# One-hot products on half the rows, with an even and an odd token side by side

## The chip, the cores and the metric

The kernel runs on one core of a Trainium2 chip. The metric is the device time of one execution in microseconds. A core has a matrix engine (PE, with its weight loads listed as PEld), a vector engine (DVE), a scalar engine (ACT), a general engine (POOL) and a queue engine (SP) that issues most transfers. All engines run on their own, each in the order of its own instruction stream, and wait for each other through semaphores.

## The reference

The input is 2048 tokens of 512 numbers. They are normalised, and two branches are added to them.

```python
xn = _layernorm(x, axis=-1)
return x + _A_ref(xn, ...) + _B_ref(xn, ...)

# A: attention, 32 query heads of 16, one shared head of keys and values
scores = einsum("bhqd,bkd->bhqk", q, k) * Dh ** -0.5
o = einsum("bhqk,bkd->bhqd", softmax(scores), v)

# B: product-key experts, 32 heads, 64 x 64 = 4096 experts
s1, s2 = q1 . k1, q2 . k2             # 64 scores each, per token and head
top_s, top_e = best 2 of the 2 x 2 sums of the two best of s1 and of s2
g = softmax(top_s)
act = gelu(einsum("nd,nhkd->nhk", xf, u[top_e]))
out = einsum("nhk,nhk,nhkd->nd", g, act, v[top_e])
```

A token uses 32 x 2 = 64 experts out of 4096. If many tokens choose, it can be cheaper to treat branch B as a dense product with a sparse gate matrix: G[token, expert] is the gate where the token chose the expert, and zero elsewhere.

## The kernel before

**Two halves of branch B.** The tokens are four groups of 512. For the first two groups (1024 tokens) the kernel gathers the rows of u and v of each chosen expert by indirect transfers (512 slots of 128 rows); DVE makes the dot product with the token (L991) and adds the weighted row to the token's total (L1026). For the last two groups it works densely (`dense`, L653): all 4096 experts in 32 blocks of 128, with matmuls pact (L733) for the activations and pout (L864) for the sums. These need the gate matrix, transposed: per block, 128 experts by 512 tokens.

**How the gates are made.** A token has 64 chosen experts. Expert e is split into a row a (0 to 127) and a block b (0 to 31), so that its gate matrix is a 128 x 32 table A^T B: A has for each of the 64 choices a one-hot row of length 128, and B a one-hot row of length 32 times the gate. The gate, scaled by 8192, is held as two f16 numbers, a high part and a remainder, so the 64 choices become 128 rows: rows 0 to 63 with the high parts, rows 64 to 127 with the remainders, and the same one-hot rows twice. `batch` (L563 on) fills three tiles `df1` (row a), `df2` (block b) and `dgt` (gates), token by token, on POOL and DVE. `spread` (L755) turns each into columns: four PE transposes of 128 x 128 into PSUM (ptd, L758) and one ACT copy to f16 into `tr` (L759). `onehot` (L782) makes, for a group of 16 tokens, the one-hot rows on DVE: a wide compare (L786, 128 x 2048), a narrow compare (L788, 128 x 512) and a multiply with the gates (L789). Then PE makes one product per token, 128 rows, 128 columns of weights, 32 streamed columns (pg, L818), all 16 tokens into one PSUM tile. Two ACT copies (L823) move that tile into a staging tile `gst`, and every 64 tokens SP stores it (L828, L830). The 512 tokens of a stage are 32 groups. The rows are prepared two groups ahead.

**What sets the order.** From the start of attention on, the order in which the instructions stand is written out by hand in one loop of rounds (`for d in range(half + 24)`). A round makes four pairs of score matmuls sc (L327) with four exponentials on ACT (L330), and 16 pv instructions (L341) for the four exponentials of the round before. There are 256 such rounds. Between the second and the third pair `mid` puts the copies of the one-hot products, the tanh of the gather part, and the dots and adds of gathered rows. At the end of a round `fill` runs the score thread: a generator that makes the expert scores psc (L531) and the dense work, and that yields a planned cost after each piece (UNIT 0.235 per matmul, 2.0 per one-hot group, 0.45 per `spread`). It is run until its cost so far reaches an aim which rises in equal parts over the 256 rounds, up to FILL. So a round holds about 3.6 units of the thread. `dense_on` tells the loop which part of the dense work is under way; while the one-hot groups run it is 2, and then the gather part advances by 1.4 slots a round.

**Buffers.** PSUM tiles of the tag x (3 buffers) serve psc, pact, pout, ptd and pg. The score tiles have two buffers of their own, so the third score pair of a round needs the first exponential to be done.

Of the kernel before, what the change touches and what calls it, by code (L numbers as in the profile page):

```python
# [23 lines left out]
P = 128  # L24
# [20 lines left out]
FILL = 948.0  # L45
# [10 lines left out]
def tile_kernel(ctx, tc, x, wq, wkv, wo, wqT, kT, uv, ub, vb, out):  # L56
# [500 lines left out]
    def dense_tiles():  # L557
        for _ in range(2):
            da = big.tile([P, 2, D], F32, name="da", tag="da", bufs=2)
            for i in range(2):  # L560
                DT.append(da[:, i, :].rearrange("p (t r s) -> p t r s", t=GT, r=2))

    def batch(ph, c, b):  # L563
# [60 lines left out]
        df1, df2, dgt = DT[:3]  # L624
# [12 lines left out]
        for r in range(2):  # L637
            G_.tensor_add(df1[:, :, r, w], hi, ii[:, 0])

        def gates():  # L640
            V.tensor_scalar(den, ex, 2.0, 2.0, op0=OP.mult, op1=OP.add)
            gg = T("gd", F32, [P, BT, 8])
            gv = gg.rearrange("p t (h k) -> p t h k", k=2)
            V.reciprocal(gv[:, :, :, 0], den)
            V.tensor_mul(gv[:, :, :, 1], ex, gv[:, :, :, 0])
            gh = T("gh", F16, [P, BT, 8])
            V.tensor_scalar(gh, gg, GS, None, op0=OP.mult)
            V.tensor_copy(dgt[:, :, 0, w], gh)
            stt(dgt[:, :, 1, w], gg, GS, gh, op0=OP.mult, op1=OP.subtract)
            if c == NC - 1:  # L650
                gated_all.append(True)
# [4 lines left out]
    def dense(DG, after):  # L656
# [62 lines left out]
        NQ = 512 // TB  # L719
# [7 lines left out]
        df1, df2, dgt = DT[:3]  # L727
# [27 lines left out]
        def spread(n):  # L755
            p = xtile("ptd")
            for j in range(GT):
                nc.tensor.transpose(p[:, j * P:(j + 1) * P], DT[n][:, j].rearrange("p r s -> p (r s)"), ident)  # L758
            nc.scalar.copy(tr[:, n, :], p)  # L759
# [3 lines left out]
        tr = kt(F16, (P, 3, 512))  # L763
# [9 lines left out]
        spread(2)  # L773
        yield 0.45
# [6 lines left out]

        def onehot(q):  # L782
            if q < NQ:
                tb = q * TB
                oa = kt(F16, shape(P))
                nc.vector.tensor_tensor(out=oa, in0=num(P), in1=bc(0, tb, P), op=OP.is_equal)  # L786
                ob = obs[:, q % 3]
                nc.vector.tensor_tensor(out=ob, in0=num(NB), in1=bc(1, tb, NB), op=OP.is_equal)  # L788
                nc.vector.tensor_mul(ob, ob, bc(2, tb, NB))  # L789
                OH[q] = oa, ob  # L790
# [15 lines left out]
        obs = kt(F16, (P, 3, TP, NB, 2))  # L806
        onehot(0)
        yield from rest_of_first
        onehot(1)
        for q in range(NQ):  # L810
            t0, ql = q // 4 * 64, q % 4
            if ql == 0:
                st = [late[0].tile([P, 16, 64], F32, name="gst", tag="wd", bufs=4) for _ in range(2)]
            onehot(q + 2)
            oa, ob = OH.pop(q)
            p = xtile("pg")
            for i in range(TB):
                nc.tensor.matmul(p[:, i * NB:(i + 1) * NB], oa[:, i // 2, :, i % 2], ob[:, i // 2, :, i % 2], start=True, stop=True)  # L818
            pv_ = p.rearrange("p (t b) -> p b t", b=NB)

            def copies(pv_=pv_, st=st, ql=ql, t0=t0):
                for hb in range(2):
                    nc.scalar.copy(st[hb][:, :, ql * TB:(ql + 1) * TB], pv_[:, 16 * hb:16 * hb + 16, :])  # L823
                if ql == 3:
# [14 lines left out]
            if q in (NQ - 16, NQ - 12):  # L839
                later_split((NQ - 16, NQ - 12).index(q))  # L840
            if q == NQ - 3:
                on_act(lambda: halves.__setitem__(2, half_split(2, 0)))
            if q == NQ - 3:
                quiet[0] = 3
            if q == NQ - 2:
# [3 lines left out]
            if q == NQ - 1:  # L849
                later_split(3)  # L850
            yield 2.0
# [519 lines left out]
```

## Time and profile before

| | before |
|---|---|
| median of 3 runs | 1915.84 us (1914.55 to 1916.74) |
| the profiled execution | 1914.46 us, span 1912.7 us |
| granted PE clock, mean | 0.984 |
| first one-hot stage | 32 groups, within 610.0 to 704.9 us |
| second one-hot stage | 32 groups, within 1409 to 1513.4 us |

The span runs from the first to the last instruction. In a row of a group, the words are line, engine, operation, output and input tiles, shapes and count, then the busy time in us and the mean of one in ns, then the idle time of the engine just before them and what ended it. In a row of windows stand the stretch, its length, busy time and count per engine, the granted clock as a share of full, the DMA share and GB/s. A row of the chain gives start, length and what ran. In a row of the timeline the start and length of a merged run of equal instructions stand first. In a row of waits stand total us, times and the longest.

### The profile page before, as it was taken

The page shows a single profiled execution, that of the slowest core. Times are in us where ns is not written, and L with a number is a line of the kernel's source. Part 1 is how long each engine was busy: PE and PEld are TensorE (multiplying, and loading weights), DVE is VectorE, ACT ScalarE, POOL GpSimd, SP SyncE. Part 2 cuts the span into 40 slices and gives each one's busy share as a digit, 9 for nine tenths or more (in the row PEclk, how much of TensorE's full clock was granted, in tenths as well). Part 3 has the DMA queues.
Part 4 walks back from the last instruction along what each step waited for, and adds up shares of the span by engine and source line. Part 5 has one row for each costly group of instructions (what it writes and reads, how often), then busy time and mean ns, then how long its engine had stood idle before and what let it go on. Part 6 is the DMA issues. An engine that isn't in the chain of part 4 may idle for free.

```text
span 1912.7 us, 35007 instructions
## 1 busy us (share of the span) xinstructions
PE 1824.5 (95%) x10990; PEld 956.9 (50%) x10990; DVE 1632.6 (85%) x6381; ACT 1290.5 (67%) x1803; POOL 693.8 (36%) x920
## 2 busy tenths in 40 slices
PE   6879999999999889999999999999998899999998
PEld 4544444555555334555555554555543345555553
DVE  6626887889998986999999897899989879999994
ACT  2336666655557987777887555555579877878873
POOL 1202433335443223344443354344522134444430
PEclk9989999999999989999999999999999999999999
DMA  7856878888673668899899987877636778899982
GB/s 263 303 201 223 289 263 299 279 290 297 223 261 122 220 222 270 247 280 296 262 288 301 377 284 241 290 248 260 237 114 228 264 227 292 269 286 279 287 274 83
DMA packets 245724, 489.76 MB, mean 256 GB/s; under 512 B 93972, under 2 KB 106644, under 8 KB 245532
## 3 DMA queue, kind: packets, MB, share of 16 engines
q0 software_dynamic: 73728, 268.47, 42.2%
q1 hardware_dynamic: 170568, 218.18, 34.8%
q8 instruction: 88, 1.44, 0.3%
q10 hardware_dynamic: 1236, 0.82, 0.1%
q14 instruction: 104, 0.85, 0.1%
HBM read 426.49 MB, written 55.61 MB: 252 GB/s over the span
## 4 chain that ended last, share of the span: by engine, by line
PE 78%; DVE 8%; ACT 2%; DMA 2%; issue 2%; SPq 0%; ACTq 0%; DVEq 0%
PE pv L341 21%; PE psc L531 18%; PE sc L327 15%; PE pact L733 9%; PE pout L864 9%; DVE oh L786 3%; PE pwo L434 2%; ACT pt L330 2%; PE pw L487 1%; DVE xa L1026 1%; DVE g L991 1%; DVE oh L789 1%; DVE oh L788 1%; DMA wqt<-in_wqT_dram 1%; DMA wk<-dw 1%
## 5 line engine op out<-in xcount | busy, mean ns | idle before, releaser
L330 ACT ACTIVATE pt<-sc 128x1024 f32<-128x1024 f32 x1024 | 994.4, 1028 | 445.7 <-PE sc L327 386.8
L979 POOL DMA_INDIRECT g<-in_uv_dram,idx x512 | 556.1, 1086 | 994.0 <-DVE xa L1026 520.2
L341 PE MATMUL pv<-pt,vaug 128*32 128x512 f32 x4096 | 505.3, 611 | 0.0
L327 PE MATMUL sc<-qa,kaug 64*128 64x512 f32 x2048 | 389.6, 453 | 15.6 <-ACT pt L330 13.3
L531 PE MATMUL psc<-wk,xt 128*128 128x512 f32 x1536 | 389.3, 401 | 4.8 <-DVE wk L497 3.6
L1026 DVE SCALAR_TENSOR_TENSOR xa<-g,w,xa 128x512 f32<-128x512 f32 x512 | 371.8, 744 | 0.1
L991 DVE CUSTOM_DVE_ANT_0 g<-g,xa 128x512 f32<-128x512 f32 x512 | 335.4, 681 | 7.0 <-DMA g<-in_uv_dram,idx 6.6
L531 PEld LDWEIGHTS psc<-wk,xt 128*128 128x128 f32 x1536 | 278.2, 188 | 108.5 <-issue 40.2
L327 PEld LDWEIGHTS sc<-qa,kaug 64*128 64x128 f32 x2048 | 158.3, 186 | 337.4 <-ACT pt L330 207.3
L341 PEld LDWEIGHTS pv<-pt,vaug 128*32 128x32 f32 x4096 | 108.2, 110 | 248.8 <-issue 247.1
L546 DVE FIND_INDEX8 i<-m,psc 128x8 uint32<-128x64 f32 x1024 | 206.4, 221 | 0.0
L733 PE MATMUL pact<-xt,wk 128*128 128x512 f32 x768 | 196.1, 400 | 0.0
L864 PE MATMUL pout<-wk,wd 128*128 128x512 f32 x768 | 194.9, 402 | 0.2 <-DVE wd L922 0.2
L544 DVE MAX8 m<-psc 128x8 f32<-128x64 f32 x1024 | 146.2, 214 | 38.7 <-PE psc L531 34.9
L864 PEld LDWEIGHTS pout<-wk,wd 128*128 128x128 f32 x768 | 140.8, 188 | 47.5 <-DVE act L991 5.5
L733 PEld LDWEIGHTS pact<-xt,wk 128*128 128x128 f32 x768 | 139.3, 188 | 48.5 <-issue 17.4
L698 DVE TENSOR_TENSOR wk<-rw,wk 128x512 fp32r<-128x512 f32 x128 | 84.9, 683 | 8.1 <-ACT wk L697 8.1
L867 DVE TENSOR_TENSOR da<-da,pout 128x512 f32<-128x512 f32 x128 | 82.8, 679 | 9.9 <-PE pout L864 9.8
L786 DVE TENSOR_TENSOR oh<-oh 128x2048 f16<-128x2048 f16 x64 | 78.0, 1219 | 0.6 <-ACT pt L330 0.4
L697 ACT CAST wk<-rw 128x512 fp32r<-128x512 f32 x128 | 74.0, 632 | 0.0
L546 DVE MATCH_VALUE_LOAD i<-m,psc 128x8 f32 x1024 | 71.0, 69 | 0.0
L590 POOL CAST fi<-i 128x64 f32<-128x64 uint32 x32 | 8.5, 266 | 152.9 <-DVE i L546 152.0
(159 smaller groups left out, 1343.4 us busy)
## 6 DMA issues: line engine op xcount, KB each, us to landing
wk<-dw SPq DMA_DIRECT2D x96, 512.0 KB
wqt<-in_wqT_dram SPq DMA_DIRECT2D x32, 512.0 KB
dw<-wk SPq DMA_DIRECT2D x32, 512.0 KB
rw<-in_ub_dram SPq DMA_DIRECT2D x64, 256.0 KB
rw<-in_vb_dram SPq DMA_DIRECT2D x64, 256.0 KB
gy<-dg SPq DMA_DIRECT2D x64, 256.0 KB
qa<-dqh SPq DMA_DIRECT2D x128, 64.0 KB
g<-in_uv_dram,idx POOLq DMA_INDIRECT x512
```

Of the source, the lines that this page charges most:

```text
L327: nc.tensor.matmul(p[:, b, :], kaug[o:o + 64, kc * P:(kc + 1) * P], QA[u][o:o + 64, i, :], start=True, stop=True)
L330: nc.scalar.activation(pt, p, AF.Exp, scale=SCALE)
L341: nc.tensor.matmul(PV[u][32 * j:32 * j + 32, :], vaug[:, kc, :], pt[:, b, :], start=kc == 0, stop=kc == 15)
L531: nc.tensor.matmul(p, XT[k][:, a, j * P:(j + 1) * P], WC[n_][k][:, bb, :], start=n == 0, stop=n == 11)
L544: nc.vector.max(m8[:, jb, s, :], p[:, s * E:(s + 1) * E])
L546: nc.vector.max_index(i8[:, jb, s, :], m8[:, jb, s, :], p[:, s * E:(s + 1) * E])
L733: nc.tensor.matmul(p, us[:, a, k * P:(k + 1) * P], XT[k][:, c, :], start=n == 0, stop=n == 11)
L786: nc.vector.tensor_tensor(out=oa, in0=num(P), in1=bc(0, tb, P), op=OP.is_equal)
L864: nc.tensor.matmul(p, wd[0][:, a, j * P:(j + 1) * P], vs[:, c, :], start=n == 0, stop=n == 5)
L979: nc.gpsimd.indirect_dma_start(out=gt, out_offset=None, in_=uv, in_offset=bass.IndirectOffsetOnAxis(ap=IDX[ph, c, ti][:, s:s + 1], axis=0))
L991: nc.vector.tensor_tensor_reduce(u, u, XN[TPH * ph + ti], scale=1.0, scalar=0.0, op0=OP.mult, op1=OP.add, accum_out=a[:, i:i + 1])
L1026: nc.vector.scalar_tensor_tensor(acc, v, w[:, i:i + 1], acc, op0=OP.mult, op1=OP.add)
```

## The change

A product gets 64 rows instead of 128. The tiles filled by `batch` hold each choice once, and the high parts and the remainders of the gates are two tiles, `dgh` and `dgl`. `spread` puts the even tokens of a pair into partitions 0 to 63 and the odd ones into 64 to 127, by matmuls with every second column of the identity (two per 128 tokens, four tiles instead of three). A group is 32 tokens: 16 steps, with an even token in the upper and an odd one in the lower half. `onehot` makes one wide compare, one narrow compare and two multiplies (with `dgh` and with `dgl`) for 32 tokens. PE makes four products per step: for each gate part r, for each half h; the two parts are added in PSUM. The two halves write two PSUM tiles. A product streams 64 columns: its own 32, and 32 more that land where the next step's product then overwrites them. Four ACT copies per group write every second token of the staging tile. The rows are prepared one group ahead, and the planned cost is 3.6 per 32 tokens instead of 2.0 per 16; FILL is 935 instead of 948.

```diff
-FILL = 948.0
+FILL = 935.0
...
-        for _ in range(2):
-            da = big.tile([P, 2, D], F32, name="da", tag="da", bufs=2)
-            for i in range(2):
-                DT.append(da[:, i, :].rearrange("p (t r s) -> p t r s", t=GT, r=2))
+        da = big.tile([P, 4, GT, 64], F32, name="da", tag="da", bufs=2)
+        DT.extend(da[:, i] for i in range(4))
...
-        for r in range(2):
-            G_.tensor_add(df2[:, :, r, w], hi, ii[:, 1])
+        G_.tensor_add(df2[:, :, w], hi, ii[:, 1])
...
-            V.tensor_copy(dgt[:, :, 0, w], gh)
-            stt(dgt[:, :, 1, w], gg, GS, gh, op0=OP.mult, op1=OP.subtract)
+            V.tensor_copy(dgh[:, :, w], gh)
+            stt(dgl[:, :, w], gg, GS, gh, op0=OP.mult, op1=OP.subtract)
...
-        NQ = 512 // TB
+        NQ = 512 // (2 * TB)
...
-                nc.tensor.transpose(p[:, j * P:(j + 1) * P], DT[n][:, j].rearrange("p r s -> p (r s)"), ident)
-            nc.scalar.copy(tr[:, n, :], p)
+                for h in range(2):
+                    nc.tensor.matmul(p[64 * h:64 * h + 64, 64 * j:64 * j + 64], DT[n][:, j, :], ident[:, h::2],
+                                     start=True, stop=True)
+            nc.scalar.copy(tr[:, n, :], p[:, :256])
...
-        spread(2)
-        yield 0.45
+        for n in (2, 3):
+            spread(n)
+            yield 0.45
...
+        def columns(ob, i, n):
+            if i % 2:
+                return ob[:, i // 2, None, :, 1].to_broadcast([ob.shape[0], n, NB])
+            return ob[:, i // 2].rearrange("p b r -> p r b")[:, :n]
...
-                ob = obs[:, q % 3]
-                nc.vector.tensor_tensor(out=ob, in0=num(NB), in1=bc(1, tb, NB), op=OP.is_equal)
-                nc.vector.tensor_mul(ob, ob, bc(2, tb, NB))
+                ob = obs[:, q % 2]
+                nc.vector.tensor_tensor(out=ob[:, 1], in0=num(NB), in1=bc(1, tb, NB), op=OP.is_equal)
+                for i in range(2):
+                    nc.vector.tensor_mul(ob[:, i], ob[:, 1], bc(2 + i, tb, NB))
...
-        onehot(1)
...
-            onehot(q + 2)
+            onehot(q + 1)
             oa, ob = OH.pop(q)
-            p = xtile("pg")
+            ps_ = [xtile("pg") for _ in range(2)]
             for i in range(TB):
-                nc.tensor.matmul(p[:, i * NB:(i + 1) * NB], oa[:, i // 2, :, i % 2], ob[:, i // 2, :, i % 2], start=True, stop=True)
+                for r in range(2):
+                    for h in range(2):
+                        o = slice(64 * h, 64 * h + 64)
+                        n = 2 if i < TB - 1 else 1
+                        nc.tensor.matmul(ps_[h][:, i * NB:(i + n) * NB], oa[o, i // 2, :, i % 2],
+                                         columns(ob[o, r], i, n), start=r == 0, stop=r == 1)
...
-                for hb in range(2):
-                    nc.scalar.copy(st[hb][:, :, ql * TB:(ql + 1) * TB], pv_[:, 16 * hb:16 * hb + 16, :])
+                for h in range(2):
+                    pb = ps_[h].rearrange("p (t b) -> p b t", b=NB)
+                    for hb in range(2):
+                        to = st[hb][:, :, ql * 2 * TB:(ql + 1) * 2 * TB].rearrange("p b (t h) -> p b t h", h=2)
+                        nc.scalar.copy(to[:, :, :, h], pb[:, 16 * hb:16 * hb + 16, :])
...
-            yield 2.0
+            yield 3.6
```

The loads and splits of the first dense blocks, which the group loop also starts, keep their places counted in tokens.

More of the change, by code (lines that the diff above doesn't have):

```diff
@@ L623, in batch @@
             dense_tiles()
-        df1, df2, dgt = DT[:3]
+        df1, df2, dgh, dgl = DT
         ii = T("ii", F32, [P, 2, BT, 8])
@@ L726, in dense @@
         yield 0.0
-        df1, df2, dgt = DT[:3]
         def activations(b, us, p):
```

25 lines of the change are left out of this document (11 added, 14 removed).

## The prediction

> **What bounds the kernel now.** I read the page's parts 1 and 2 first, then the chain of work that ended last, then stretches of it.
>
> ```profile
> span 1912.7 us, 35007 instructions
> PE 1824.5 (95%) x10990; PEld 956.9 (50%) x10990; DVE 1632.6 (85%) x6381; ACT 1290.5 (67%) x1803; POOL 693.8 (36%) x920
> PE   6879999999999889999999999999998899999998
> DVE  6626887889998986999999897899989879999994
> PEclk9989999999999989999999999999999999999999
> ```
>
> PE is the bound nearly everywhere. It dips in slices 13 and 14 and again near 30 and 31, and those are the two stretches in which the dense gates are made from one-hot products. The change lies there. The same stretches by windows, with an ordinary one as the third row, and then the pv matmuls (L341) alone in the first two:
>
> ```profile
> 610.00:704.90 94.90, 78.88 (x906) 34.25 (x904) 92.96 (x189) 85.39 (x143) 21.27 (x18) 0.95 0.64 208
> 1417.30:1513.40 96.10, 81.23 (x906) 34.66 (x904) 94.15 (x191) 85.56 (x144) 23.70 (x20) 0.91 0.67 222
> 842.00:1043.00 201.00, 200.39 (x1139) 110.25 (x1137) 192.29 (x445) 161.20 (x230) 85.65 (x76) 1.00 0.89 283
> ...
> 610.00:704.90 94.90, 36.74 (x272) 7.57 (x272) 0.95 0.64 208
> 1417.30:1513.40 96.10, 39.06 (x272) 7.77 (x272) 0.91 0.67 222
> ```
>
> The busy columns are PE, PEld, DVE, ACT, POOL. In the one-hot stretches DVE is busy 98% of the time, ACT 89 to 90%, PE 83 to 85%, and the granted clock falls to 0.95 and 0.91. One round of attention holds 16 pv instructions, so 272 of them are 17 rounds: 34 rounds in 191.0 us, 5.62 us each. Who waits there, and the chain:
>
> ```profile
> PE pg L818 <- DVE oh L789: 9.2, 12, 1.4
> ACT pt L330 <- PE sc L327: 7.6, 10, 1.5
> ...
> 611.83 1.14 DVE oh L786
> 613.76 1.14 DVE oh L786
> 615.69 1.14 DVE oh L786
> ```
>
> PE waits for the one-hot rows; the chain goes from one L786 to the next every 1.93 us. So this stage is bound by DVE, with ACT close behind. Now an ordinary round, from the chain:
>
> ```profile
> 560.85 1.85 PE pv L341 x16
> 562.70 0.66 PE sc L327 x4
> 563.37 3.63 PE psc L531 x15
> 566.99 0.66 PE sc L327 x4
> 567.66 1.85 PE pv L341 x16
> ```
>
> It takes 6.81 us, all PE: 3.17 us of attention (1.85 + 2 x 0.66) and 3.63 us of the score thread. The 256 rounds are fixed, and so is the thread's work outside the one-hot stages. A shorter one-hot round gains its whole shortening. But one-hot rounds fewer in number push their attention into PE-bound rounds, at 3.17 us each.
>
> **Part by part: the products on PE.** Before, 32 tokens are 32 matmuls; after, 64, each of 64 rows and 64 columns, each with its own weight load.
>
> ```profile
> 622.98 0.57 PE L818 MATMUL pg<-oh 128*128 128x32 f16 x16
> 617.70 0.96 PE L818 MATMUL pg<-oh 128*128 128x32 f16 x32
> 560.12 0.30 PEld L327 LDWEIGHTS sc<-qa,kaug 64*128 64x128 f32 x4 [0.35 <-issue]
> 560.78 0.16 PEld L341 LDWEIGHTS pv<-pt,vaug 128*32 128x32 f32 x8 [0.36 <-issue]
> L327 PEld LDWEIGHTS sc<-qa,kaug 64*128 64x128 f32 x2048 | 158.3, 186 | 337.4 <-ACT pt L330 207.3 <-issue 111.0 <-ACT wk L697 5.0
> ```
>
> (0.96 - 0.57) / 16 is 24 ns, rounded 25 ns per product with its load. No row shows an f16 product on half the rows. Cheap end: two halves run side by side, as the pairs of L327 do (four loads of 186 ns within 0.30 us), so 32 pairs at 25 ns: 0.8 us. Dear end: the loads keep L327's pace, second pair 0.30 - 0.19 = 0.11 us after the first: 32 x 0.11 = 3.5 us. I take 25 ns for each of the 64, 1.6 us, because L818 is the nearest row: same type, same 128 weight columns, same pattern. PE per round: 3.17 + 1.6 + 0.1 for changing over = 4.87 us.
>
> The Trainium skill, "TensorEngine Tiling (Array Packing)", section Performance Considerations, says a small matmul costs some 60 cycles whatever its length, and that one should not tile a dimension that is already small: twice as many of them cost twice as much, the 1.6 us. "TensorE: Matmul & The Clock Gate", Part 3, has matmuls of different row groups start 4 ns apart, by which a pair would cost about 29 ns, 32 pairs 0.93 us, and the sum below would be some 3 us better, ACT then being the limit.
>
> **DVE.** Per 32 tokens two L786, two L788 and two L789 become one wide compare, one narrow compare and two multiplies.
>
> ```profile
> 614.82 0.42 DVE L788 TENSOR_TENSOR oh<-oh 128x512 f16<-128x512 f16 x1
> 615.27 0.42 DVE L789 TENSOR_TENSOR oh<-oh 128x512 f16<-128x512 f16 x1
> 615.61 1.22 DVE L786 TENSOR_TENSOR oh<-oh 128x2048 f16<-128x2048 f16 x1
> L991 DVE CUSTOM_DVE_ANT_0 g<-g,xa 128x512 f32<-128x512 f32 x512 | 335.4, 681 | 7.0 <-DMA g<-in_uv_dram,idx 6.6 <-issue 0.4
> L1026 DVE SCALAR_TENSOR_TENSOR xa<-g,w,xa 128x512 f32<-128x512 f32 x512 | 371.8, 744 | 0.1
> ```
>
> From start to start: 1.14 + 0.45 + 0.34 = 1.93 us before; 1.14 + 0.45 + 2 x 0.34 = 2.27 us after, instead of 3.86 us. The gather work keeps the planner's rate of 1.4 slots a round: at most 1.4 x (0.68 + 0.74) = 2.0 us. So 4.3 us a round: DVE stops being the limit. A group is now prepared one group ahead instead of two, but one group fills a round, so the lead in time stays.
>
> **ACT.** The copies stay four per 32 tokens and of the same size; their output now steps over every second column.
>
> ```profile
> 1420.93 1.84 ACT pt L330 x2
> 1432.33 0.55 ACT gst L823 x2
> L823 ACT COPY gst<-pg 128x256 f32<-128x256 f32 x128 | 43.9, 421 | 0.0
> L1007 ACT ACTIVATE gth<-gy 128x4 f32<-128x4 f32 x128 | 27.5, 215 | 0.5 <-DVE gy L1001 0.5
> ```
>
> Four exponentials at 0.92, four copies at 0.275, and 0.08 of tanh: 4.86 us. I cost the stride at nothing: L823's copies, 421 ns each, already read PSUM with a stride. A 20% dearer copy would add 0.2 us a round. The copies of one round now stand together ahead of its third exponential, and they release the two of three PSUM buffers that each group takes; the next products come after two more score pairs, by when the first copies are done.
>
> PE 4.87, ACT 4.86, DVE 4.3. What is left of waiting: L330 waits for L327 for 7.6 us in 17 rounds, 0.45 each, and part of that is DVE's doing; I take 0.2 (bounds 0 and 0.45). A one-hot round is then 5.1 us (4.9 to 5.35).
>
> **The rest.** In the changed program's order, 32 rounds hold a group, against 34, and one round in the second stage holds no thread work: it costs ACT's 4.8 us. So 33 rounds against 34, and the one left over becomes an ordinary one: 3.17 us more attention in PE-bound time. The transposes:
>
> ```profile
> L758 PE MATMUL ptd<-ident,da 128*128 128x128 f32 x24 | 3.4, 279 | 2.0 <-ACT oh L759 1.3 <-ACT pt L330 0.7
> L487 PE MATMUL pw<-wqt,kTs 128*64 128x512 f32 x128 | 38.2, 673 | 8.4 <-PEq L266 5.5 <-issue 2.3 <-DMA wqt<-in_wqT_dram 0.6
> ```
>
> 12 a stage at 0.142 (3.4 / 24) are 1.7 us. After, 32 f32 products of 64 columns, two instructions each if they go as L487's (128 for 64 matmuls). Low: 64 x 0.298 / 8 = 2.4 us; high: 64 x 0.142 = 9.1 us. I take 2.7, near L487's kind: +1.0 a stage, +2 in all, up to +15. Four f16 casts of 256 columns replace three of 512 on ACT: nothing. POOL drops two small adds a batch, off the path: nothing. FILL 935 for 948 follows the thread's total, which falls by 2 x (64 - 57.6 - 0.45) = 11.9 units: both programs end the thread in the same round, nothing. The queues of SP carry the same gate stores.
>
> Sum: 32 x 5.1 + 4.8 + 3.2 + 2.0 - 191.0 = 163.2 + 10.0 - 191.0 = -17.8 us. The profiled execution took 1914.46 us by its own time, 1.4 under the median of the runs shown: 1914.46 - 17.8 = 1896.7, and 1898 against the median of 1915.84.
>
> **Rivals.** (1) Half-row loads are slow: this ends on the other side. The place is PE in the one-hot rounds. At 3.5 us a group PE needs 6.8 us a round: 32 x 6.8 + 10 - 191 = +37 us, 1952. It breaks even where a round takes 181/32 = 5.66 us; less 3.27 and the 0.2 of waiting that is 2.2 us a group, 34 ns a product. For it: L327's half-row loads are no shorter than full ones, and twice as many are issued. Against it: those are f32 and L818 loads 128 columns of f16 within its 25 ns. The Trainium skill, "TensorE: Matmul & The Clock Gate", section LDWEIGHTS, has load time depend on columns and not on rows, so halving the rows saves nothing; the two kinds of load here agree with that as far as they go.
>
> (2) The clock still drops. Clock 0.95 and 0.91 cost 0.05 x 94.9 + 0.09 x 96.1 = 13 us of PE work, hidden today under DVE. If the drops stay they are no longer hidden, PE being a limit: -18 + 13 = -5 us, 1911. Against it: PE would be busy about 95% of a round instead of 84%. More waiting for PSUM or copies (round 5.5 us) ends at the same place.
>
> (3) PE is cheaper, 0.8 us a group: ACT alone limits, round 4.9 to 5.0, about -22 us, 1894. The change cannot fail to do what it says on DVE: the compares are gone.
>
> **How the numbers follow.** My forecast 0.57 (own range 1891 to 1905), (3) 0.08, (2) 0.16 (1904 to 1919), (1) 0.19 (1918 to 1952). A measurement of this kernel tells 0.2%, 3.8 us, from no change. Faster: 0.57 + 0.08 and two thirds of (2), 0.11: 0.76. Same: the rest of (2) and a little of (1), 0.07. Slower: 0.17. The range 1889 to 1922 takes in the forecast, (3), (2) and the mild part of (1); what is left out is the rest of (1), some 0.13, and 0.04 below.
>
> **What would show it.** Right: pg products starting 25 ns apart, 64 in about 1.6 us; rounds with products of about 5.1 us; DVE under 90% in them and no wait of pg for oh; clock near 1.00. Wrong: a group of over 2.2 us, pg waiting for copies, copies longer than 0.42 us, clock under 0.95, or transposes (ptd) of over 5 us a stage.

## The result and the profile after

The changed kernel takes 1939.62 us (1938.29 to 1941.37) against 1915.59 us (1914.55 to 1916.74) for the kernel before (the three runs of the table above and a fourth): a ratio of 1.0122, interval 1.0109 to 1.0135. The forecast was 1898 with a range of 1889 to 1922; it is off by 42 us and wrong in its sign. The profiled execution took 1938.29 us, its span is 1936.6 us.

The first three lines of the page of the changed kernel that answer to those shown of before (span, busy time, PE in 40 slices):

```profile
span 1936.6 us, 37163 instructions
PE 1833.4 (95%) x12118; PEld 963.5 (50%) x12118; DVE 1587.0 (82%) x6317; ACT 1291.1 (67%) x1805; POOL 678.2 (35%) x888
PE   6879999999999889999999899999998899999998
```

DVE lost 46 us of work, as meant, and it bought nothing. Now the windows over the one-hot stages, cut at rounds: rounds 64 to 81 and 182 to 199. (A round is taken to start with the first of its 16 pv matmuls, L341. The columns are as before: stretch, length, busy time of PE, PEld, DVE, ACT, POOL, granted clock, DMA share, GB/s.) First the kernel before, then the changed one:

```profile
602.30:704.90 102.60, 85.88 (x951) 38.13 (x949) 98.51 (x203) 91.95 (x152) 25.83 (x25) 0.95 0.64 206
1402.30:1507.50 105.20, 90.33 (x947) 40.01 (x945) 97.53 (x220) 91.36 (x150) 27.88 (x35) 0.92 0.59 195
```

```profile
602.00:708.10 106.10, 91.91 (x1547) 43.73 (x1547) 78.31 (x199) 93.19 (x156) 26.01 (x32) 0.95 0.62 202
1417.20:1524.60 107.40, 91.54 (x1498) 44.68 (x1497) 82.65 (x248) 90.72 (x149) 27.74 (x33) 0.98 0.57 188
```

DVE falls from 98.5 to 78.3 us and from 97.5 to 82.7, and the stretches do not get shorter: +3.5 and +2.2 us. PE stood still for 102.60 - 85.88 = 16.7 and 14.9 us before, and for 14.2 and 15.9 us after. Where the rest of the 24 us lies follows from the starts of the rounds in the two traces: rounds 82 to 91 +2.6 us, rounds 128 to 136 +6.2, rounds 137 to 181 +2.8, rounds 200 to 206 +5.4. Over two thirds of the loss against the kernel before lie outside the one-hot stages. The forecast, however, had these stages some 18 us shorter, so of the 42 us by which it missed about half lie in them.

Two things in the trace are new. The first is at the end of the first dense stage, rounds 132 and 133. One row of the waits, one of the chain of that stretch and three of PE's timeline:

```profile
DVE gy L917 <- DMA gy<-dg: 6.2, 1, 6.2
...
1055.09 11.09 DMA gy<-dg
...
1063.13 1.65 PE L874 MATMUL pout<-wk,wd 128*128 128x512 f32 x6
1066.95 3.07 PE L874 MATMUL pout<-wk,wd 128*128 128x512 f32 x12 [2.16 <-DVE gy L917]
...
1078.04 3.35 PE L874 MATMUL pout<-wk,wd 128*128 128x512 f32 x7 [2.93 <-DVE wd L932]
```

The gate rows of one block, whose transfer is issued at 1055.09, arrive 11.09 us later; DVE stands at L917 for 6.2 us, and PE waits 2.16 and then 2.93 us for what comes out of it. Before, these two rounds took 6.19 and 7.78 us; now 10.00 and 11.86. The second is in the products themselves. PE's timeline through one group, here from the last occasion on which the changed kernel ran (a5_after, which shows the same as the first profile):

```profile
1465.05 0.96 PE L826 MATMUL pg<-oh 64*128 64x64 f16 x42
1466.50 0.26 PE L826 MATMUL pg<-oh 64*128 64x64 f16 x5 [0.50 <-issue]
1467.26 0.26 PE L826 MATMUL pg<-oh 64*128 64x64 f16 x5 [0.50 <-issue]
1468.02 0.33 PE L826 MATMUL pg<-oh 64*128 64x64 f16 x5 [0.51 <-issue]
1468.76 0.32 PE L826 MATMUL pg<-oh 64*128 64x64 f16 x7 [0.41 <-issue]
```

After 42 products PE gets only five every 0.75 us, and waits for nothing that the profile shows ("issue"). Added up over the first profile, the starts of neighbouring products of one group that lie more than 100 ns apart make 17.0 us of gaps, in 16 of 32 groups. These are of two kinds. 12.9 us, in 11 groups, lie inside the stream, as in the five rows above; these are called interruptions from here on. The other 4.1 us, in five groups, lie behind the first product, and there, in four of the five, the profile shows what PE waits for: the second PSUM tile of the group is not free before ACT has copied it out. Two rows of PE's timeline (first profile, round 200), and PE's idle time before products over all groups, from the view of the tile pg:

```profile
1526.99 0.20 PE L826 MATMUL pg<-oh 64*128 64x64 f16 x1
1528.61 1.12 PE L826 MATMUL pg<-oh 64*128 64x64 f16 x63 [1.42 <-ACT gst L834]
...
  issue: 8.0, 16
  ACT gst L834: 3.0, 4
```

### The profile page after: what moved, and what is told of

It is laid out like the page before. It is cut to its first block, busy times and chain, and to the rows that moved or that the text cites. A ratio compares the mean times of both kernels' runs of the same rounds, so it can differ in the third digit from the quotient of the medians.

```text
span 1936.6 us, 37163 instructions
## 1 busy us (share of the span) xinstructions
PE 1833.4 (95%) x12118; PEld 963.5 (50%) x12118; DVE 1587.0 (82%) x6317; ACT 1291.1 (67%) x1805; POOL 678.2 (35%) x888
## 4 chain that ended last, share of the span: by engine, by line
PE 76%; ACT 6%; DVE 5%; issue 3%; DMA 2%; SPq 0%; ACTq 0%; DVEq 0%; POOL 0%
PE pv L341 21%; PE psc L531 18%; PE sc L327 15%; PE pact L728 8%; PE pout L874 8%; ACT pt L330 5%; PE pwo L434 2%; PE pw L487 2%; DVE xa L1036 1%; DMA gy<-dg 1%; DVE g L1001 1%; ACT gst L834 1%; PE pg L826 1%; DMA dg<-gst 0%; PE pwl L409 0%
## 5 line engine op out<-in xcount | busy, mean ns | idle before, releaser
L341 PE MATMUL pv<-pt,vaug 128*32 128x512 f32 x4096 | 504.1, 609 | 0.0
L341 PEld LDWEIGHTS pv<-pt,vaug 128*32 128x32 f32 x4096 | 108.1, 110 | 249.1 <-issue 247.5
L1024 DVE SCALAR_TENSOR_TENSOR w<-gth,ga 128x4 f32<-128x4 f32 x128 | 20.6, 161 | 89.9 <-ACT gth L1017 87.5
```

Source lines behind the costliest of these rows:

```text
L341: nc.tensor.matmul(PV[u][32 * j:32 * j + 32, :], vaug[:, kc, :], pt[:, b, :], start=kc == 0, stop=kc == 15)
```

## The experiments

Two theories at the start. **Interruption**: the products stop in some groups, and without that the forecast would have come true. **Plan**: the shifted costs (3.6 a group, FILL 935) put other work in the wrong rounds. A third came up on the way, **floor**: a round cannot be shorter than 4.9 us, whatever is taken from it.

### The products alone

The kernels of this part and of the next ones ran on four chips, called B to E here; which of the chips gave the first profile is not known. The four kernels of this part ran once each; ten runs of the changed kernel on chip C lie between 1903.34 and 1917.78 us, so differences of a few us between single values say nothing, and what is read here is read from the traces. e1_again is the changed kernel unaltered, on chip B (the kernel before took 1904.93 us there, a single value).

> The changed kernel unaltered, profiled a second time. What it tells apart: stalls that belong to the program from stalls that come and go. The first profile of the change has, beside the one-hot stages, three long rounds near 1061 to 1136 us: PE and DVE wait for one gate transfer (6.2 us) and ACT stands 6.4 us without a releaser. If they belong to the program, they are back within 2 us of their place and size and the time is 1936 to 1942 us. If they are chance, the rounds from 1054 to 1137 us take about 10 us less and the time is about 1928 us.

It took 1909.53 us, with gaps of 4.2 us in total instead of 17.0, and all but 0.2 us of them are the waits for copies. The 16 rounds of the first stage took 82.5 us, 5.16 each. So the interruptions are not in the program alone, and the one-hot rounds of the first stage come out as forecast; but no gain is seen (the two single values lie 4.6 us apart, the wrong way). The stall in rounds 132 and 133 is there again (12.77 and 8.39 us), and the time is 18 us and more under both values that were expected.

e2_batched issues the gathers of the one-hot rounds eight at a time every fourth round, since the interrupted groups were those beside a gather on POOL.

```diff
-                    gathers(4)
+                    if dense_on[0] != 2:
+                        gathers(4)
+                    elif d % 4 == 0:
+                        gathers(8)
```

> In the one-hot stages the gathers on POOL are issued only in every fourth round, up to eight at once, instead of one or two each round; all else stays. Theory A (PE's burst of 128 instructions is slowed while POOL issues gathers): of the 32 groups, 22 or more show no gap over 0.1 us between products, against 16 in the first profile; the gaps sit in the rounds with gathers, and the two stages together take 5 to 12 us less than 188 us. Theory B (PE runs out of instructions by itself, whatever POOL does): as many groups with gaps as before, 14 to 18, spread over rounds with and without gathers, stages within 3 us of 188 us.

1908.59 us, gaps 3.3 us, of which 0.2 us inside the stream. Where nothing is interrupted there was nothing to win, so it tells nothing on the cause.

e3_high_only leaves out the remainders of the gates: half of the products.

```diff
-                for r in range(2):
+                for r in range(1):
...
-                                         columns(ob[o, r], i, n), start=r == 0, stop=r == 1)
+                                         columns(ob[o, r], i, n), start=True, stop=True)
```

> The products with the remainders of the gates are left out, so a group is 32 matmuls instead of 64 and the gates have their high part alone. Theory B (PE's instruction supply is what stalls): a burst of 64 instructions as the kernel before had; no gap over 0.1 us that is not a wait for copies, groups of 0.45 to 0.5 us, rounds of 4.9 us nearly throughout, stages together 165 to 172 us instead of 188 us. Theory C (the long rounds come from the halved PE clock, which follows low PE activity): the halved stretches become more, not fewer, granted clock under 0.94 in the stages, and the stages gain under 6 us.

1910.6 us, no better. PE's timeline through two rounds shows why:

```profile
655.08 0.64 PE L826 MATMUL pg<-oh 64*128 64x64 f16 x32
656.18 0.50 PE L327 MATMUL sc<-qa,kaug 64*128 64x512 f32 x2 [0.46 <-ACT pt L330]
657.10 0.49 PE L327 MATMUL sc<-qa,kaug 64*128 64x512 f32 x2 [0.41 <-ACT pt L330]
657.52 1.92 PE L341 MATMUL pv<-pt,vaug 128*32 128x512 f32 x16
659.38 0.73 PE L327 MATMUL sc<-qa,kaug 64*128 64x512 f32 x4
659.95 0.64 PE L826 MATMUL pg<-oh 64*128 64x64 f16 x32
```

From one group to the next 659.95 - 655.08 = 4.87 us, with PE waiting 0.46 and 0.41 us for exponentials. What the products no longer take, PE waits longer. In the changed kernel a round without any thread work (round 187) takes 4.88 us too. The chain of such a round: the last exponential frees a score tile, a score pair, 16 pv instructions, the third pair, and two exponentials.

e4_32_columns streams the 32 columns of a product only, without the 32 that are overwritten.

```diff
-                        n = 2 if i < TB - 1 else 1
+                        n = 1
```

> Each product streams its own 32 columns only, without the 32 that are overwritten. If the 25 ns from start to start of the kernel before is a floor per pair of halves, pairs start every 25 ns instead of 29 ns, groups take 0.8 us instead of 0.95 us, and nothing else moves: time within 4 us of the change. Theory C (clock follows PE activity): the granted clock in the stages falls under 0.94 and 0.97 of the first profile, and the time rises by 3 us or more. If the second 32 columns cost supply time, the gaps get fewer.

1913.34 us. A group takes 0.8 us instead of 0.95, and no gain is seen, as a floor would have it.

### The floor

e5_pv_split puts the second half of the pv instructions behind the fourth score pair, so that the chain from exponential to exponential holds 8 of them and not 16.

```diff
             pv(pu, pk)
-            pv(pu, pk + 1)
-            if pk == 14:
-                unit_tail(pu)
         mid()
         if i < STEPS:
             scores(u, kc + 1, 0)
             scores(u, kc + 1, 1)
+        if 0 < i <= STEPS:
+            pv(pu, pk + 1)
+            if pk == 14:
+                unit_tail(pu)
```

> The changed kernel with the 16 pv instructions of a round in two halves: eight where all stood, eight behind the third and fourth score pair. Theory F (a round cannot be shorter than 4.88 us because of attention's own loop, one score pair, all of pv, the next score pair, two exponentials, whatever the products cost): the loop loses 0.93 us, the round without thread work falls from 4.88 to 3.8 to 4.2 us, rounds with products fall to 4.7 to 4.8 us where ACT alone is the limit, PE-bound rounds stay 6.81 us; 4 to 8 us less than the change. Theory G (the 4.88 us are ACT's four exponentials and four copies): no round falls under 4.8 us, the one without thread work neither, and the time stays within 2 us of the change.

2078.09 us, ratio 1.0856 (1.083 to 1.0881): in an ordinary round the pv instructions had covered two exponentials, and now they don't. Its waits of PE between 800 and 900 us:

```profile
PE sc L327 <- ACT pt L330: 5.4, 13, 0.4
```

An ordinary round takes 7.65 us instead of 6.81; 0.41 us of the 0.84 us is this wait, the rest was not taken apart. In the one-hot stages the edit shows what it was made for: the round without copies on ACT (188) falls from 4.88 to 4.45 us (3.8 to 4.2 were expected), rounds with copies stay at 4.8 to 5.9, and the mean of the first stage rises from 5.16 to 5.27. e6_copy_dve has this split too, and moves one of the four copies of a group to DVE.

```diff
-                        nc.scalar.copy(to[:, :, :, h], pb[:, 16 * hb:16 * hb + 16, :])
+                        if h == 1 and hb == 1:
+                            nc.vector.tensor_copy(to[:, :, :, h], pb[:, 16 * hb:16 * hb + 16, :])
+                        else:
+                            nc.scalar.copy(to[:, :, :, h], pb[:, 16 * hb:16 * hb + 16, :])
```

> As the kernel with pv in two halves, and one of the four copies of a group goes to DVE. By theory F ACT is then at 4 x 0.92 + 3 x 0.275 + 0.08 = 4.6 us and DVE at about 4.7 us: rounds with products 4.6 to 4.75 us, 2 to 5 us less than with pv in two halves alone. By theory G the copies are the limit and rounds fall by 0.275 us each, 9 us over 32 rounds, whether or not pv is split.

2072.85 us, ratio 1.0836 (1.0813 to 1.0858), for the same reason. Some one-hot rounds now take 4.52, 4.60 and 4.59 us (68, 76, 78; 4.91, 4.85 and 4.87 with the split alone), the mean of the first stage is 5.08. So two limits lie at the same 4.9 us: the chain, and ACT's own four exponentials and four copies. Neither is worth breaking at that price.

### Without interruptions: no difference

b0_before and a0_after are the two kernels unaltered, together on chip C, where e5_pv_split and e6_copy_dve ran too.

> The kernel before, unaltered, profiled where the change is profiled too. Theory D (most of the gain that was forecast was time which the first profile of the kernel before lost to the halved clock and not to DVE): the 34 rounds of the two one-hot stages take 172 to 180 us here instead of 191 us, most of them 4.9 to 5.3 us, and the clock in the stages is over 0.96. Theory E (the gain is real in the stages and is lost elsewhere): the 34 rounds take 188 us or more.

> The changed kernel unaltered, timed against the kernel before. Repeating the second profile: rounds of 4.88 us with some of 5.4 to 6 us, the first stage's 16 rounds in 82.5 us, and a time of 0.1 to 0.4% over the kernel before. Repeating the first: groups with gaps of 0.7 us between products, 91 us, and 1.0 to 1.4% over it.

b0_before: 17 rounds in 95.0 and 17 in 95.8 us, so the 191.0 us of the forecast stand. a0_after: 1911.79 us, ratio 0.9998 (0.998 to 1.0017), with gaps of 5.6 us, 0.2 us of them inside the stream. The time that PE stands still, worked out from the two traces by rounds (length less the union of PE's instructions), in us:

| rounds | before: length, idle | after: length, idle |
|---|---|---|
| 1 to 63 | 452.6, 8.7 | 456.3, 11.7 |
| 64 to 81 | 102.7, 17.5 | 97.4, 11.0 |
| 82 to 127 | 321.1, 1.6 | 320.3, 1.5 |
| 128 to 136 | 64.6, 1.1 | 70.3, 5.7 |
| 137 to 181 | 311.1, 0.0 | 309.0, 0.0 |
| 182 to 199 | 103.9, 14.8 | 99.8, 10.9 |
| 200 to 206 | 48.3, 2.1 | 52.9, 3.7 |

PE's busy time is the same in both (1819.1 and 1819.8 us), so all that the change can give is idle time: 32 us were there in the stages, 10.4 of it went, and 9.2 came back: 7.6 us in rounds 1 to 63 and 128 to 136, in places that the products do not touch, and 1.6 us in rounds 200 to 206, where the last group waits 2.89 us for copies behind its first product.

### The plan

Four kernels together, again on chip C, the changed one as the measure (a2_after). a1_pace_before keeps the new products and takes back the planned cost and the aim:

```diff
-FILL = 935.0
+FILL = 948.0
...
-            yield 3.6
+            yield 4.0
```

c1_cost30 and c2_cost24 go the other way, to more than one group a round, with FILL lowered by as much: cost 3.0 and FILL 915.8, cost 2.4 and FILL 896.6.

> The changed kernel unaltered, as the measure for the three beside it. If the 16 interrupted groups of the first profile (17.0 us of gaps between products) belong to the program, they return and the time is 1.0 to 1.3% over the kernel before. If they belong to the occasion, gaps are under 6 us in total, the time is within 0.3% of before, and PE is idle 11 us in each one-hot stage (rounds 64 to 81 and 182 to 199) and 5 to 6 us in rounds 128 to 136, as in the other two looks.

> The new products at the pace of the kernel before: cost 4.0 a group instead of 3.6 and FILL 948 instead of 935, so that 32 groups again take 34 rounds (rounds 74 and 193 hold no thread work) and the rounds just behind them hold 1.4 to 5.0 units instead of 0.7 to 6.8. If the uneven rounds (82 to 87, 184, 200 to 205) are what ate the gain: rounds 200 to 206 take 48 us as before instead of 52 to 53, and the time is 5 to 8 us under the unaltered changed kernel. If PE's idle time is only moved: the two empty rounds take 4.88 us each of which 1.7 is idle, the idle time of the stages stays at 11 us each, and the time is within 3 us of the changed kernel.

> A group is booked at 3.0 units (FILL 915.8, lower by 32 x 0.6), so that a one-hot round holds 1.2 groups on average (every fifth holds two). If the floor of 4.88 us a round is what limits a round with one group (PE's own work there is 4.2 us), fewer such rounds mean less idle: 16 rounds x 0.7 becomes some 13 x 0.7, 9 us a stage instead of 11, and the time is 2 to 5 us under the changed kernel. If products, copies or DVE limit, rounds with two groups take over 7 us and nothing is gained.

> The same at 2.4 units (FILL 896.6): every second one-hot round holds two groups. By the floor: a round with one group 4.9, with two 3.17 + 2.1 = 5.3 on PE and 3.9 + 8 x 0.275 = 6.1 on ACT; 16 groups in 5.3 rounds of each kind take 59 us, and PE is idle 5.3 x (0.7 + 0.9) = 8 us a stage: 4 to 7 us under the changed kernel. If what limits is the one-hot rows on DVE (2.3 us a group and up to 2.0 us of gather work a round), a round with two takes 6.6 us and the gain is under 3 us; if it is the copies that free the two PSUM tiles, it takes over 7 us and the time is no better.

| | median us | ratio to before (1909.46) |
|---|---|---|
| a2_after | 1910.94 | 1.0007 (0.9989 to 1.0025) |
| a1_pace_before | 1899.88 | 0.9952 (0.9934 to 0.9969) |
| c1_cost30 | 1918.62 | 1.0043 (1.0021 to 1.0064) |
| c2_cost24 | 1910.38 | 1.001 (0.9994 to 1.0026) |

Two constants are worth 11 us. a1_pace_before spreads its 32 groups over 34 rounds, as the kernel before did, and is faster than both kernels. Its rounds 200 to 206 take 47.2 us (54.7 in a2_after, whose traced run is 11 us over its median; 51.8 to 52.9 in e1_again, a0_after and a3_after), its rounds 1 to 63 452.2 (456.5). Against my expectation the idle time of its one-hot stages is no worse than in a2_after (11.3 and 10.9 against 10.9 and 11.6 us), empty rounds included. Two groups in a round do not pay either (2 to 5 and 4 to 7 us of gain were expected); the waits of PE in the first stage of c2_cost24:

```profile
PE pg L826 <- DVE oh L794: 7.4, 6, 1.9
PE sc L327 <- ACT pt L330: 5.1, 12, 0.7
```

The one-hot rows are prepared one group ahead, and the second group of a round waits for them, up to 1.9 us.

### The exchange of products and plans

b2_plan_after is the fourth combination: the kernel before, with the plan of the changed one.

```diff
-FILL = 948.0
+FILL = 935.0
...
-            yield 2.0
+            yield 1.8
```

Beside it, on chip D, both of the new kernels again and a pace between them (f_cost39: cost 3.9, FILL 944.8).

> The other half of the exchange: the old products (128 rows, groups of 16 tokens) with the plan of the changed kernel, FILL 935 and cost 1.8 for 16 tokens. If the plan by itself costs time: idle time of PE of over 2 us appears in rounds 14 and 29 and over 5 us in rounds 128 to 136, as in the changed kernel and not as in the kernel before, and the time is 5 to 12 us over the kernel before. If the plan hurts only together with the new products, rounds 1 to 63 and 128 to 136 take as long as in the kernel before and the time is within 3 us of it.

> The new products at the pace of the kernel before (cost 4.0, FILL 948) once more. If its gain is the plan's, it is again 0.3 to 0.7% under the kernel before and 8 to 12 us under the unaltered changed kernel; if it was the occasion, the interval takes in 1.

> The changed kernel unaltered, on the chip of this call. If the interruptions between products of the first profile (17.0 us in 16 groups) come with some chips, they may come back here: then 1.0 to 1.3% over the kernel before, and the same kernel at cost 4.0 and FILL 948 beside it is also interrupted, which would make the gaps independent of the plan. Otherwise within 0.3% of the kernel before, with under 7 us of gaps.

> Cost 3.9 and FILL 944.8: a pace between the two, with rounds 65 and 184 holding 6.2 units and rounds 201 to 203 2.1 to 4.3. If evenness behind the stages is what counts, rounds 200 to 206 take 48 us as before and the time is within 4 us of that with cost 4.0. If any shift of the plan can put a transfer behind its user, some stall that neither has appears in rounds 1 to 63 or 128 to 136, and the time lies between the two, 1902 to 1908.

| median us (ratio) | plan of before | plan of after |
|---|---|---|
| old products | 1910.65 | 1932.97 (1.0111, 1.0083 to 1.0139) |
| new products | 1900.9 (0.9938, 0.9918 to 0.9958) | 1914.09 (1.0011, 0.9997 to 1.0025) |

f_cost39 took 1904.04 (0.9974, 0.9959 to 0.9989); of what was expected both came in part, since its rounds 200 to 206 take 48.4 us, but its rounds 128 to 136 take 70.8. The new products are worth 9.8 us with the old plan and 18.9 with the new; the new plan costs 22.3 us with the old products and 13.2 with the new. The idle time of over 2 us in rounds 14 and 29 is in both kernels with FILL 935, whichever products they have, and in neither with FILL 948 (which has one of 2.26 us in round 23 instead; over rounds 1 to 63 the new products take 452.2 us with FILL 948 and 458.5 with 935). In the first profile of the changed kernel these are, from the waits of PE in two stretches:

```profile
PE pwt L494 <- DVE i L546: 2.3, 1, 2.3
...
PE psc L531 <- DVE wk L497: 2.7, 1, 2.7
PE pwt L494 <- DVE i L546: 1.1, 1, 1.1
```

They lie 200 us and more ahead of the first one-hot product. Rounds 128 to 136 are less clean: 64.6 us in b0_before, 69.7 in b2_plan_after, 67.4 in a4_pace_again, 68.2 in a3_after. My expectation of over 5 us of idle time there in b2_plan_after did not hold (3.9 us), and its whole time lies ten us above what I had expected, since the old one-hot rows make the rounds of a tighter plan wait. What the new products take away is seen in the first stage, windows of rounds 64 to 81 under the same (new) plan, b2_plan_after and then a3_after, and the waits of PE for rows in b2_plan_after:

```profile
600.30:711.90 111.60, 91.77 (x983) 41.77 (x981) 102.26 (x233) 95.45 (x159) 27.14 (x34) 0.92 0.59 190
...
PE pg L818 <- DVE oh L789: 13.8, 14, 1.4
```

```profile
602.40:699.80 97.40, 86.42 (x1547) 42.44 (x1545) 78.06 (x199) 92.53 (x156) 26.08 (x32) 1.00 0.67 219
```

14.2 us shorter, the clock 1.00 instead of 0.92, and the wait for rows is gone.

### The aim alone, and the interruptions once more

d1_fill941 is the changed kernel with FILL 941 and the cost left at 3.6; a5_after the changed kernel unaltered, on chip E.

> The changed kernel with FILL 941 instead of 935 and the cost of 3.6 a group kept: only the aim moves, by 0.6%. If the time hangs on where single pieces of the thread fall among the rounds (which the aim alone sets in rounds 1 to 63), the idle time of PE in rounds 14, 15, 28, 29 and 132, 133 changes place or size without the products being touched, by 3 us or more in all, and the time moves by 3 to 10 us from the unaltered changed kernel, either way. If only the booked cost matters, the time stays within 3 us of it.

> The changed kernel unaltered on the chip of this call. If the interruptions between products (17.0 us in the first profile) come with the chip or the occasion, this is one more draw: either 1.0 to 1.3% over the kernel before with over 10 us of gaps, or within 0.3% with under 7 us. In both cases the stalls in rounds 14, 29 and 132 to 133 are there, since they belong to the plan.

a5_after: 1934.81 us, ratio 1.0117 (1.0092 to 1.0141), gaps of 16.9 us: the first result come back. d1_fill941: 1933.83, ratio 1.0113 (1.0086 to 1.0139), gaps of 17.0 us; it lost the stalls of rounds 200 to 206 (47.8 us instead of 51.1) and got a worse one in round 132 (17.79 us; 7.57 in a5_after). The aim alone moves stalls about by several us each, here with no gain in the sum: the stalls moved as in the first of the two outcomes expected, the time stayed as in the second.

| occasion | changed kernel / before | gaps behind the first product (waits for copies), us | gaps inside the stream (interruptions), us | groups beside a gather that are interrupted |
|---|---|---|---|---|
| first profile | 1.0122 | 4.1 | 12.9 | 10 of 12 |
| e1_again | 1909.53 / 1904.93, single | 4.0 | 0.2 | 0 of 18 |
| a0_after | 0.9998 | 5.4 | 0.2 | 0 of 18 |
| a2_after | 1.0007 | 6.3 | 0.2 | 0 of 18 |
| a3_after | 1.0011 | 4.1 | 0.2 | 0 of 16 |
| a5_after | 1.0117 | 3.7 | 13.2 | 10 of 11 |

On two occasions the program is interrupted, in the same ten rounds; on four (chips B, C and D) it is not. All ten groups stand beside a gather. Of the groups without a gather only one has a gap inside the stream, of 0.2 us in round 185, and it has it in all six traces. A lowered clock is not what stops the products: during all ten groups of the first profile the granted clock was 1.00. What "beside a gather" means is seen in POOL's timeline of a5_after, to be held against the five rows of PE shown above:

```profile
1464.42 1.20 POOL L989 DMA_INDIRECT g<-in_uv_dram,idx  x1 [8.71 <-DVE xa L1036]
1465.93 0.96 POOL L989 DMA_INDIRECT g<-in_uv_dram,idx  x1 [0.30 <-issue]
1467.20 1.18 POOL L989 DMA_INDIRECT g<-in_uv_dram,idx  x1 [0.30 <-issue]
```

and a group beside a gather in a3_after, first POOL, then PE:

```profile
1497.80 1.15 POOL L989 DMA_INDIRECT g<-in_uv_dram,idx  x1 [4.40 <-DVE xa L1036]
```

```profile
1497.72 1.12 PE L826 MATMUL pg<-oh 64*128 64x64 f16 x64
```

64 products without a gap. The old products (16 to a group) are not interrupted in any of the three traces that have them; but two of these come from chips C and D, where the new ones are not interrupted either, and the chip of the third is not known. That the kernel before takes 1912.18 us on chip E and 1910.65 on chip D speaks for the old products, and no trace of them from chip E shows it.

## Why the prediction was wrong

**The step that failed first: "FILL 935 for 948 follows the thread's total ... both programs end the thread in the same round, nothing."** It looked at where the thread ends and not at what it meets on the way. The plan by itself costs 13.2 us with the new products and 22.3 with the old ones. Its parts as the traces of the new products show them, the changed kernel unaltered against a1_pace_before and a4_pace_again: rounds 1 to 63 take 3 to 6 us more (455.1 to 458.5 against 452.2), rounds 128 to 136 1 to 4 (68.2 to 71.0 against 67.3 and 67.4), rounds 182 to 199, where nothing is interrupted, 1 to 5 (99.8 to 103.0 against 97.8 and 98.6), and rounds 200 to 206 4 to 8 (51.1 to 54.7 against 47.2). A part of the last is a wait for copies: the last group, in round 200, stands 1.0 to 4.1 us behind its first product, and 0.8 in a4_pace_again. With the old products 18 us lie in the two stages (111.6 and 113.0 us against 102.7 and 103.9 in b0_before). Which of the two constants does it was not separated.

**What was left out: that the products could be held up on their way to PE.** Rival (1) had the right place (PE in the one-hot rounds; 4 of 32 groups of the first profile took over 2.2 us by interruptions) and the wrong cause: not the load of half-rows, but a stream that stops beside a gather. That 1939.62 us lies within its 1918 to 1952 is luck. Between a3_after and a5_after, the same program on two chips, lie 1934.81 - 1914.09 = 20.7 us, while the kernel before differs by 1.5. Of that 13.2 - 0.2 = 13.0 us are the interruptions themselves, and 4.5 us rounds 137 to 181 (313.5 against 309.0 us). There round 140 alone takes 11.24 us instead of 6.81; in the first profile it takes 11.66, in this wait of ACT:

```profile
ACT pt L330 <- issue: 6.4, 1, 6.4
```

This, too, is a wait for nothing that the profile shows. What is left of the 20.7 us, some 3 us, was not taken apart; the clock of the first stage is lower, 0.94 here against 1.00 in a3_after (windows of a5_after, rounds 64 to 81):

```profile
601.40:709.60 108.20, 93.67 (x1543) 44.06 (x1542) 78.07 (x199) 93.06 (x156) 26.05 (x32) 0.94 0.62 198
```

Together: 10 us won by the products at the old plan, 13 lost by the plan, some 20 lost on an occasion with interruptions. That makes about 23, and 24 were measured; that the three add up on one chip was not measured.

Point by point, the rest of the forecast:

- **Products on PE, 1.6 us a group: too dear.** Undisturbed, the two halves of a step mostly start 3 to 4 ns apart and the next pair 29 ns later in the median: 64 products in 0.95 us. That was rival (3). The Trainium skill, "TensorE: Matmul & The Clock Gate", Part 3, lets products of different row groups start some 4 ns apart; the trace agrees, with 3 to 4 ns. It changed nothing: by e3_high_only half of the products take as long a round as all.
- **A one-hot round of 5.1 us: right in the first stage only.** There it is 5.16 without interruptions (82.5 us for 16). In the second stage the forecast had 16 x 5.1 + 4.8 = 86.4 us, and rounds 184 to 200 take 94.1 to 97.3 us in the four traces without interruptions, as long as in b0_before (95.8); with the old plan they take 89.7 and 90.6. How much of the excess is thread work that the plan moved into round 184 (9.14 us in a0_after, 5.67 in a1_pace_before) was not taken apart. The bound of 4.86 that the forecast gave ACT is right in size, but the chain through 16 pv instructions gives the same 4.88 without any copy. The kernel before already had rounds of 4.88 among its 5.62 on average, so only its slower rounds had anything to give.
- **The copies done before the next products: wrong for 4 of 32 groups.** In rounds 72, 80, 192 and 200 the second product waits for them, by 0.7 to 0.8 us from start to start in the first three and 1.0 to 4.1 us in the last. The forecast named this as a sign of being wrong. In round 200 the copies in their turn wait for the store of the staging tile; this row is from the waits of a2_after, 1500 to 1516 us:

```profile
ACT gst L834 <- DMA dg<-gst: 3.1, 2, 2.1
```

- **DVE under 90%: right** (78.31 of 106.10 us is 74%), and PE's wait for rows is gone.
- **Clock near 1.00: right without interruptions in the first stage** (a3_after 1.00; 0.97 in its second), wrong in the first profile (0.95 and 0.98). With the old plan it is 0.98 in both stages (a4_pace_again), so interruptions are not its only cause.
- **Transposes 2.7 us a stage: right in size.** 128 instructions of 64 columns in both stages:

```profile
L754 PE MATMUL ptd<-ident,da 128*64 128x64 f32 x128 | 4.7, 224 | 2.2 <-ACT oh L756 2.2
```

- **Copies with a stride, nothing: off by a tenth.** L834 takes 459 ns on average, L823 took 421; in a round of 4.88 us that does not show.
- **The sum, -17.8: too large.** It was set against the kernel before with the plan of before, and by that measure the new products are worth 9.8 us: of 32 us of idle time in the two stages (b0_before) 21 us are still there in a4_pace_again, in rounds at the floor and in the waits for copies. That they are worth 18.9 us under the new plan comes near the forecast by luck: it is measured against old rows that the tighter plan makes wait, which the forecast did not speak of.

Open: what interrupts the products, and whether it is the chip or the occasion. It was not tried to take the gathers out of the one-hot rounds where the stream is interrupted; e2_batched ran where there was nothing to see. Nor did the new products run with the old plan on chip E, so whether they gain anything there is not known. In the trace of a5_after no block of PE's instructions was under way during the gaps of 9 of the 10 interrupted groups; so a block in flight is not what it shows. The Trainium skill, "Runtime: NRT & Kernel Launch", section "Instruction fetch mechanics", says that instructions are fetched in blocks of 16 KiB while earlier ones run, and that this is hidden by the pace of dispatch; the 128 instructions of a group here go out in 0.95 us, 7 ns each, and no run here shows whether that is too fast for the supply on some chips. Also open: why the gate transfer of rounds 132 and 133 takes 11.09 us here and 5.87 us in a4_pace_again.

## What to carry to other kernels

Before a limit is taken away, read how long the engine that ends the program stands still in that stage: here 32 us of 207 (rounds 64 to 81 and 182 to 199), and a floor of 4.88 us a round left two thirds of it standing. A change of a planned cost or an aim re-deals all later work and some of the earlier, so measure the new code with the old plan first; here, on chips C and D, the old plan made of a draw a gain of 0.5 to 0.6%. And run on more than one chip before believing a 1% loss: a burst of short instructions was fluent on three chips and interrupted on two occasions.

## What the runs showed of the hardware

- Two f16 products of 64 rows each with their own loads, in the upper and the lower half, mostly start 3 to 4 ns apart, 29 ns from pair to pair in the median: 64 in 0.95 us from the first start to the last, 1.12 us to the last end (the row of a3_after above). 32 products of 128 rows take 0.97 us to the last end in b0_before.
- The same program lost 13 us in interruptions of its product stream on two occasions and 0.2 us on four others. In the group shown the interrupted stream gives five products every 0.75 us. 10 of 12 and 10 of 11 of the groups beside a gather on POOL are hit on the two occasions, none of 16 to 18 on the four; the granted clock was 1.00 in all ten of the first profile.
- On all six occasions the group waits in four rounds (72, 80, 192, 200) for the ACT copies that free its second PSUM tile; the gaps behind a first product make 3.7 to 6.3 us in all.
- Splitting 16 pv instructions into 8 and 8 cost 0.84 us in each of the ordinary rounds (7.65 against 6.81), of which 0.41 us is PE's wait for an exponential that they had covered.
